# Last output block copied in halves by two engines, and two output blocks stored by one DMA

## The chip, the cores and the metric

The kernel runs on one core of a Trainium2 chip. The metric is the time of one execution on the device in microseconds; lower is better. TensorE (PE) multiplies matrices and leaves the results in PSUM, an accumulator memory of eight banks. VectorE (DVE), ScalarE (ACT) and GpSimd (POOL) do the rest, and SyncE (SP) issues the transfers between the chip's working memory and HBM. The transfers are carried out by 16 DMA engines.

## The reference

Four sequences of 768 positions go through a linear attention with a decaying state (8 heads of 48), and its result, viewed as 768 rows of 384 values per sequence, through a gated long convolution. In short:

```python
# attention: state is updated at each position t
y[t]  = r[t] @ (state + (u * k[t]) outer v[t])
state = w[t] * state + k[t] outer v[t]
# gated convolution over the sequence, per sequence x = y of all heads side by side
x1, x2, x3 = split(x @ w_proj, 3)                      # 384 columns each
x2c = irfft(rfft(x2) * rfft(filter))                   # along the 768 positions
out = (x1 * x2c * x3) @ w_out                          # 768 x 384, float32
```

The inputs and the output are float32; the output has 4 x 768 x 384 values.

## The kernel before, in words

Each sequence (batch index 0 to 3) is cut into six row blocks of 128 positions. The attention runs block by block over 24 blocks in all; the convolution is done with matrices of sines and cosines on TensorE. Work of one sequence's convolution overlaps with the attention of the next ones, so only the convolution of the last sequence (index 3) is left for the end of the program.

There is no scheduler. The order is written out by hand in the string ORDER, one word for each step: the engine's letter (P for TensorE, A for ScalarE, V for VectorE, G for GpSimd, S for the queue of SP), the step and its indices, and behind an @ the PSUM bank. Each engine carries out its words in the order in which they stand. The waits between engines are put in by the framework, from which tile each instruction reads and writes; the order does not name them.

The steps that the change and the prediction touch are at the end of the program, for sequence 3:

- `yl` and `yh` (lines 817 and 822) multiply the convolution's result by the gate, the left and the right half of the positions, for each of three column groups. Their results are the left factors of the output product.
- `pA.3.t` (line 835) starts the output product of row block t with the first two column groups; `pB.3.t` (line 842) adds the third. `pA.3.4` is special: it makes one PSUM tile of two banks in the pool `wide`, and puts row block 4 into its first bank and row block 5 into its second. The other blocks have a bank each.
- `o.3.t` (the copy helper, line 276 on ScalarE and 278 on VectorE) copies row block t, 128 partitions by 384 float32 values, from PSUM into the tile `o_all`, which holds six such blocks. The previous sequence used the same tile, so a copy must also wait until the old block's store has landed.
- `st.3.t` (line 859) stores row block t of `o_all` to HBM with one DMA of 192 KB on the queue of SP.

The last words of the order for ScalarE are the copies of blocks 2, 1, 5, 3 and 4; VectorE copies block 0. The last stores are those of blocks 2, 1, 5, 3, 4 and 0, in this order. When the last has landed, the engines pass a closing barrier and the program ends.

Of the kernel before, what the change touches and what calls it, by code (L numbers as in the profile page):

```python
# [19 lines left out]
B, H, S, D = 4, 8, 768, 48  # L20
L = 128
NCH = S // L
C = H * D
# [112 lines left out]
P:po.2.3@3 V:s.3.0 V:s.3.1 P:iE.3.2@2 G:yl.3.0 A:o.2.3 P:iO.3.2@5 V:d.3.0 A:o.2.1 P:iP.3.2  # L136
S:st.2.3 V:yl.3.1 G:yh.3.0 P:po.2.5@3 S:st.2.1 V:d.3.1 A:ec.3.2 P:po.2.4@4 A:o.2.5 V:s.3.2
P:pA.3.1@1 A:o.2.4 S:st.2.5 P:pA.3.2@0 V:yl.3.2 V:yh.3.1 S:st.2.4 P:pB.3.2 V:d.3.2 P:pB.3.1
P:pA.3.4@8 A:o.3.2 V:yh.3.2 A:o.3.1 S:st.3.2 P:pB.3.4 S:st.3.1 P:pA.3.3@2 A:o.3.5 P:pB.3.3
P:pA.3.0@3 A:o.3.3 S:st.3.5 P:pB.3.0 A:o.3.4 V:o.3.0 S:st.3.3 S:st.3.4 S:st.3.0  # L140
"""


# [1 line left out]
def kernel(  # L145
# [12 lines left out]
    nc = tc.nc  # L158
# [54 lines left out]
    o_all = consts.tile([L, NCH, C], FP32)  # L213
# [39 lines left out]
    bank_of = {}  # L253
# [20 lines left out]
    def copy(e, o, i):  # L274
        if e == "A":
            nc.scalar.activation(out=o, in_=i, func=AF.Copy)  # L276
        elif e == "V":
            nc.vector.tensor_copy(out=o, in_=i)  # L278
        else:
            nc.gpsimd.tensor_copy(out=o, in_=i)  # L280
# [574 lines left out]
    def op_o(e, b, ti):  # L855
        copy(e, o_all[:, ti, :], bank_of[f"po.{b}.{ti}"])

    def op_st(e, b, ti):
        nc.sync.dma_start(out=out[b, ti * L:(ti + 1) * L, :], in_=o_all[:, ti, :])

# [71 lines left out]
```

## Time and profile before

| | |
|---|---|
| time, median of 3 runs | 156.67 us (156.21 to 157.68) |
| the profiled execution's own time | 157.1 us |
| its span, from the first to the last instruction | 155.4 us |
| mean granted TensorE clock | 0.973 |
| DMA queues: bytes moved | 28.98 MB, mean 186 GB/s |
| stores of the output | 24 of 192 KB each, median 2.2 us from issue to landing |

The profile shows one execution. Its times are in microseconds from the span's start, and a row of the timeline gives start, duration, engine, line, operation, the tile written and the tiles read. In brackets stands how long the engine was idle before, and what ended the idle time. SPq is the queue of SP: the duration of its rows is the time to issue a transfer, not the transfer. PE, DVE, ACT and POOL are TensorE, VectorE, ScalarE and GpSimd. The profiled execution is one of many, so a sum made from its rows is made against its own 155.4 and 157.1 us, and is then set beside the median.

### The profile page before, as it was taken

To read this page: it belongs to the slowest core of one execution; us is meant where nothing else is said; L and a number is where in the kernel's file an instruction comes from. 1 tells how busy PE (TensorE), PEld (TensorE's weight loads), DVE (VectorE), ACT (ScalarE), POOL (GpSimd) and SP (SyncE) were. 2 spreads that over 40 slices of the span, in tenths; PEclk is the share of its full clock that TensorE was granted. 3 is DMA by queue.
4 is the path that set the end of the run, shared out by engine and by line. 5 is a ranking of instruction groups with operands and counts; after the bars stand their busy time and mean duration, and the time that the engine had idled before them with its cause. 6 is when DMAs were issued, how large, how long until landed. Compare 5 with 4: busy or idle time off the path is not lost.

```text
span 155.4 us, 4177 instructions
## 1 busy us (share of the span) xinstructions
PE 144.5 (93%) x1540; PEld 90.8 (58%) x1540; DVE 138.3 (89%) x264; ACT 128.2 (82%) x306; POOL 115.9 (75%) x134
## 2 busy tenths in 40 slices
PE   6969988968999999999999999999999999999990
PEld 3446565756465666656757666775666566555440
DVE  6537879979989999999999999999999989999950
ACT  3279659969698899989999999999999877677470
POOL 7200869892999899799969999699999998900600
PEclk9985799999999999999999999999999999999997
DMA  5999979999999999899999999978999986000575
GB/s 96 196 202 183 207 148 197 195 286 226 244 172 281 253 178 200 170 192 211 190 200 259 170 181 210 189 147 141 227 209 228 206 175 222 2 0 0 181 281 203
DMA packets 112038, 28.98 MB, mean 186 GB/s; under 512 B 106641, under 2 KB 112018, under 8 KB 112018
## 3 DMA queue, kind: packets, MB, share of 16 engines
q1 hardware_dynamic: 112018, 28.72, 84.4%
q8 instruction: 12, 0.20, 0.6%
q14 instruction: 8, 0.07, 0.1%
HBM read 22.41 MB, written 4.72 MB: 175 GB/s over the span
## 4 chain that ended last, share of the span: by engine, by line
PE 63%; DMA 12%; DVE 11%; ACT 5%; SPq 5%; issue 2%; DVEq 0%
PE p L705 13%; DMA ldw<-in_w_dram 9%; PE x L735 6%; PE po L850 6%; PE f L421 5%; SPq L452 5%; PE sc L607 3%; PE f L413 3%; PE tqk L588 3%; DMA ldv<-in_v_dram 3%; PE iE L792 3%; PE iO L781 3%; PE iE L781 2%; PE yt L675 2%; DVE mt L614 2%
## 5 line engine op out<-in xcount | busy, mean ns | idle before, releaser
L505 POOL TENSOR_TENSOR qk<-ldr,eq 128x384 bf16<-128x384 f32 x20 | 21.3, 1067 | 11.4 <-ACT F L357 10.3
L705 PE MATMUL p<-xT,wproj 128*128 128x384 bf16 x144 | 29.3, 326 | 0.1
L614 DVE TENSOR_TENSOR mt<-sc,mask_excl 128x1024 bf16<-128x1024 f32 x24 | 29.2, 1216 | 0.0
L502 POOL TENSOR_TENSOR qk<-ldk,en 128x384 bf16<-128x384 f32 x21 | 22.4, 1067 | 4.1 <-PE kv L625 2.7
L508 POOL TENSOR_TENSOR rk<-ldr,ldk 128x384 bf16<-128x384 f32 x19 | 19.8, 1042 | 1.8 <-issue 1.5
L560 POOL TENSOR_TENSOR rku<-rk,u_bc 128x384 bf16<-128x384 bf16 x19 | 18.0, 945 | 2.5 <-DVE rk L508 1.3
L462 ACT ACTIVATE lg<-ldw 128x384 bf16<-128x384 f32 x24 | 12.6, 530 | 8.6 <-DMA ldw<-in_w_dram 7.5
L705 PEld LDWEIGHTS <-wproj 128*128 128x128 bf16 x144 | 13.0, 97 | 8.2 <-issue 1.0
L582 POOL TENSOR_TENSOR vc<-v,cc 128x384 bf16<-128x384 bf16 x19 | 16.5, 867 | 0.7 <-DVE cc L566 0.5
L757 DVE TENSOR_TENSOR filt<-f,HF 128x768 bf16<-128x768 f32 x18 | 16.6, 952 | 0.1
L735 PE MATMUL x<-wproj,sd 128*128 128x384 bf16 x72 | 14.9, 326 | 0.3 <-DVE HF L435 0.2
L276 ACT ACTIVATE qkT<-tqk 128x1024 bf16<-128x1024 bf16 x13 | 13.3, 1027 | 0.1
L276 ACT ACTIVATE v<-ldv 128x384 bf16<-128x384 f32 x23 | 12.2, 530 | 1.3 <-DMA ldv<-in_v_dram 1.3
L276 ACT ACTIVATE x<-p 128x384 bf16<-128x384 f32 x24 | 11.7, 499 | 1.8 <-PE p L705 1.6
L726 POOL TENSOR_TENSOR g<-g,x 128x384 bf16<-128x384 bf16 x8 | 7.1, 912 | 8.1 <-DVE g L278 8.1
L276 ACT ACTIVATE ab<-x 128x384 bf16<-128x384 f32 x24 | 11.7, 500 | 1.2 <-PE x L735 0.9
L484 ACT ACTIVATE en<-cs 128x384 f32<-128x384 f32 x24 | 11.9, 500 | 0.9 <-PE cs L466 0.7
L490 ACT ACTIVATE eq<-ce 128x384 f32<-128x384 f32 x24 | 11.5, 494 | 0.6 <-PE ce L478 0.6
L588 PE MATMUL tqk<-ident,qk 128*128 128x128 bf16 x144 | 11.5, 230 | 0.2 <-ACT phi L496 0.2
L632 DVE TENSOR_TENSOR S<-kv,phi 128x384 bf16<-128x384 f32 x20 | 10.9, 550 | 0.3 <-PE kv L625 0.2
L566 DVE TENSOR_REDUCE cc<-rku 128x8 f32<-128x384 bf16 x21 | 11.1, 541 | 0.0
L276 ACT ACTIVATE xT<-yt 128x384 bf16<-128x384 bf16 x20 | 9.9, 495 | 1.3 <-PE yt L675 0.6
(158 smaller groups left out, 397.0 us busy)
## 6 DMA issues: line engine op xcount, KB each, us to landing
ldw<-in_w_dram SPq DMA_DIRECT2D x24, 192.0 KB, 4.0
ldk<-in_k_dram SPq DMA_DIRECT2D x24, 192.0 KB, 4.2
ldr<-in_r_dram SPq DMA_DIRECT2D x24, 192.0 KB, 3.9
ldv<-in_v_dram SPq DMA_DIRECT2D x24, 192.0 KB, 4.0
out_dram<-o_all SPq DMA_DIRECT2D x24, 192.0 KB, 2.2
raw<-in_moe_w_proj_dram SPq DMA_DIRECT2D x3, 576.0 KB, 5.8
filt<-in_moe_filter_fft_dram SPq DMA_DIRECT2D x1, 1152.0 KB
P<-in_moe_w_out_dram SPq DMA_DIRECT2D x1, 576.0 KB, 5.0
```

The source lines that it names most:

```text
L276: nc.scalar.activation(out=o, in_=i, func=AF.Copy)
L462: nc.scalar.activation(out=o, in_=i, func=AF.Ln)
L502: two(e).tensor_mul(qk_b[c % 3][:, 1, :, 0:D], ld["k"][c % 6], en_b[c % 3])
L505: two(e).tensor_mul(qk_b[c % 3][:, 0, :, 0:D], ld["r"][c % 6], eq_b[c % 3])
L508: two(e).tensor_mul(rk_b[c % 2], ld["r"][c % 6], ld["k"][c % 6])
L560: two(e).tensor_mul(rku_b[c % 2], rk_b[c % 2], u_bc)
L582: two(e).tensor_mul(o, v, s.to_broadcast([L, H, D]))
L588: nc.tensor.transpose(p[:, x, j, :], qk_b[c % 3][:, x, 2 * j:2 * j + 2, :], ident)
L614: nc.vector.tensor_mul(mt_b[c % 3], bank_of[f"sc{c}"].rearrange("p q j t -> p (q j) t"), dataclasses.replace(m[:, :], ap=[m[:, :].ap[0], [ ...
L705: nc.tensor.matmul(p, wproj[:, cb, col0:col0 + L], xT_b[b % 2][:, cb, sl], start=(cb == 0), stop=(cb == CB - 1),)
L735: nc.tensor.matmul(p, sd_b[q][0][:, cb, ti * L:(ti + 1) * L], wproj[:, cb, C:2 * C], start=(cb == 0), stop=(cb == CB - 1),)
L757: two(e).tensor_mul(U_all[:, part, n], dataclasses.replace(f, ap=[f.ap[0], [0, 2]] + list(f.ap[1:])), HF[:, n, part:part + 2, :],)
```

## The change

The last words of the order are rewritten, and two steps are added. `oh` copies one half of the columns (192 of 384) of a row block; `sp` stores row blocks 4 and 5 of a sequence with one DMA of 384 KB.

- Block 5 is copied by VectorE instead of ScalarE (`V:o.3.5`).
- ScalarE copies block 4 ahead of block 3 instead of behind it.
- Blocks 4 and 5 are stored by one DMA (`S:sp.3`), which stands ahead of the store of block 3.
- Block 0 is copied in two halves, the left by ScalarE, the right by VectorE.

```diff
-P:pA.3.4@8 A:o.3.2 V:yh.3.2 A:o.3.1 S:st.3.2 P:pB.3.4 S:st.3.1 P:pA.3.3@2 A:o.3.5 P:pB.3.3
-P:pA.3.0@3 A:o.3.3 S:st.3.5 P:pB.3.0 A:o.3.4 V:o.3.0 S:st.3.3 S:st.3.4 S:st.3.0
+P:pA.3.4@8 A:o.3.2 V:yh.3.2 A:o.3.1 S:st.3.2 P:pB.3.4 S:st.3.1 P:pA.3.3@2 V:o.3.5 A:o.3.4 P:pB.3.3
+P:pA.3.0@3 S:sp.3 A:o.3.3 P:pB.3.0 S:st.3.3 A:oh.3.0.0 V:oh.3.0.1 S:st.3.0
...
+    def op_oh(e, b, ti, n):
+        sl = slice(n * (C // 2), (n + 1) * (C // 2))
+        copy(e, o_all[:, ti, sl], bank_of[f"po.{b}.{ti}"][:, sl])
+
+    def op_sp(e, b):
+        nc.sync.dma_start(
+            out=out[b, 4 * L:, :].rearrange("(a p) c -> p a c", p=L), in_=o_all[:, 4:, :]
+        )
```

## The prediction

> **What bounds the kernel now.** I read the page first, then the chain that ended last, because the change touches only the last two lines of the written order. The page says that over the whole span several engines are nearly full:
>
> ```profile
> span 155.4 us, 4177 instructions
> PE 144.5 (93%) x1540; PEld 90.8 (58%) x1540; DVE 138.3 (89%) x264; ACT 128.2 (82%) x306; POOL 115.9 (75%) x134
> ```
>
> These shares say nothing about the tail, which has limits of its own. The end of the chain, in order of time (start, duration, what):
>
> ```profile
> 150.68 0.33 PE pA L835 x2
> 151.00 0.18 PE pA L842
> 151.18 0.02 issue
> 151.20 0.56 DVE o_all L278
> ```
>
> The chain as printed stops at the last copy, 151.76, but the span runs 3.6 us further. So the next views were the timeline of each engine in that stretch, the queue's own waits, and busy time by short stretches. Here are the last copies, with the last two VectorE multiplies before them (start, duration, engine, line, operation):
>
> ```profile
> 148.43 0.35 DVE L822 TENSOR_TENSOR raw<-raw,g 128x384 bf16<-128x384 bf16 x1
> 149.28 0.36 DVE L822 TENSOR_TENSOR raw<-raw,g 128x384 bf16<-128x384 bf16 x1
> 149.69 0.50 PE L842 MATMUL pA<-wout,raw 128*128 128x384 bf16 x2
> 150.30 0.49 ACT L276 ACTIVATE o_all<-pA 128x384 f32<-128x384 f32 x1 [0.39 <-PE pA L842]
> 150.72 0.49 ACT L276 ACTIVATE o_all<-pA 128x384 f32<-128x384 f32 x1
> 151.10 0.48 ACT L276 ACTIVATE o_all<-pA 128x384 f32<-128x384 f32 x1
> 151.20 0.56 DVE L278 COPY o_all<-pA 128x384 f32<-128x384 f32 x1 [1.57 <-PE pA L842]
> ```
>
> ScalarE copies row blocks 5, 3 and 4 one behind the other (150.30, 150.72, 151.10), VectorE copies block 0. Each is followed by its store on SP's queue:
>
> ```profile
> 150.81 0.33 SPq L859 DMA_DIRECT2D out_dram<-o_all  x1
> 151.24 0.38 SPq L859 DMA_DIRECT2D out_dram<-o_all  x1
> 151.71 0.40 SPq L859 DMA_DIRECT2D out_dram<-o_all  x1
> 152.21 0.41 SPq L859 DMA_DIRECT2D out_dram<-o_all  x1
> ```
>
> The first is issued 0.02 us after the copy of block 5 ends (150.79). The last is issued 0.45 us after its copy ended (151.76), so it waited for SP, which needs 0.43 to 0.50 us from one store to the next. Whether SP or the engines that move the data set the end is seen in the stretches (engine columns, then granted clock, DMA share, GB/s):
>
> ```profile
> 148.80:149.15 0.35, 0.35 (x4) 0.22 (x3) 0.35 (x1) 0.16 (x1) 0.00 (x0) 1.00 0.04 13
> 149.15:150.20 1.05, 1.05 (x8) 0.43 (x7) 0.45 (x2) 0.76 (x2) 0.00 (x0) 1.00 0.96 358
> 151.40:151.60 0.20, 0.00 (x0) 0.00 (x0) 0.20 (x1) 0.19 (x1) 0.00 (x0) 1.00 0.26 85
> 151.60:151.80 0.20, 0.00 (x0) 0.00 (x0) 0.16 (x1) 0.00 (x0) 0.00 (x0) 1.00 0.68 253
> 151.80:153.60 1.80, 0.00 (x0) 0.00 (x0) 0.00 (x0) 0.00 (x0) 0.00 (x0) 1.00 1.00 367
> 153.60:153.80 0.20, 0.00 (x0) 0.00 (x0) 0.00 (x0) 0.00 (x0) 0.00 (x0) 1.00 0.88 346
> 153.80:154.00 0.20, 0.00 (x0) 0.00 (x0) 0.00 (x0) 0.00 (x0) 0.00 (x0) 0.58 0.11 31
> ```
>
> Near 151.6 the DMA engines are almost out of work (share 0.26); from about 151.65 to 153.83 they are full at 367 GB/s and empty after that. Summing these rows from 151.60 on gives 50.6 + 660.6 + 69.2 + 6.2 = 787 KB, which is four stores of 192 KB (196.6 thousand bytes each). So the four last stores leave no gap: **the tail is bound by the bytes, counted from the moment the first of the four stores is issued.** The landing times confirm it (the store's issue with min/median/max in ns, then us from issue to landing):
>
> ```profile
> L859 SPq DMA_DIRECT2D out_dram<-o_all x1: 332/332/332, 150.8 to 150.8; - x1
> DMA to landing us min/median/max: 1.9/1.9/1.9
> ...
> L859 SPq DMA_DIRECT2D out_dram<-o_all x2: 399/406/412, 151.7 to 152.2; - x2
> DMA to landing us min/median/max: 2.1/2.1/2.1
> ...
> L927 SPq EVENT_SEMAPHORE  x7: 17/28/28, 154.3 to 155.3; - x7
> ```
>
> The first of the four lands 1.9 us after its issue, the last two after 2.1: each queues a little behind the one before. The last lands at 152.21 + 2.1 = 154.31, and there the closing steps of SP begin. From the first issue to the last landing it is 154.31 - 150.81 = **3.50 us**; the remaining 1.1 us to the span's end is closing work that the change does not touch.
>
> **The change part by part.** Nothing ahead of the last two lines of the order moves; the first 150.2 us stay as they are, and TensorE's instructions are the same to the end.
>
> *Block 5 to VectorE.* VectorE is free from 149.28 + 0.36 = 149.64. The two last matmuls that write blocks 4 and 5 begin at 149.69 and end at 150.19. The copy also needs the old store from this row block to have landed; that was issued at 148.32, 1.9 us earlier than 150.22:
>
> ```profile
> 148.32 0.33 SPq L859 DMA_DIRECT2D out_dram<-o_all  x1
> ```
>
> So VectorE starts at about 150.25 and, at the 0.56 us of the same copy of block 0, ends at 150.81. ScalarE's copy ended at 150.79, so this edit is nearly free by itself.
>
> *Block 4 behind block 5.* The two blocks lie in one PSUM tile of two banks, and in the changed program as built ScalarE's copy of block 4 waits for VectorE's counter at the very value that the copy of block 5 raises. The copies that look parallel run one after the other. The hand-over from VectorE costs about 0.05 us (multiply ends 149.64, the matmul behind it starts 149.69), up to the 0.11 between matmul end 150.19 and copy start 150.30. Block 4 therefore starts at 150.81 + 0.07 = 150.88 and ends, at 0.49, at 151.37. Queued behind it on ScalarE are block 3 and the half of block 0. Were the wait not there, block 4 would still need its old store, issued third from last before the tail, to land:
>
> ```profile
> 148.74 1.10 SPq L859 DMA_DIRECT2D out_dram<-o_all  x2
> ...
> L859 SPq DMA_DIRECT2D out_dram<-o_all x4: 332/358/402, 148.7 to 150.8; - x4
> DMA to landing us min/median/max: 1.9/1.9/2.0
> ```
>
> That is 150.64 to 150.74, so it could start at 150.76 and end at 151.25 at best. This is the low bound for this step.
>
> *One store for blocks 4 and 5.* Today's store of block 5 goes out at 150.81, while block 4 is still uncopied. The paired store must wait for both and goes out at 151.37 + 0.02, say 151.40: **0.59 us later** (0.46 at the low bound). The engines have nothing else to move by then, so the short gap at 151.5 grows by as much. An operation like the pair has no row in this trace. Its issue lies between one block (0.33) and the three blocks of a weight load:
>
> ```profile
> L386 SPq DMA_DIRECT2D P<-in_moe_w_out_dram x1: 672/672/672, 79.9 to 79.9; - x1
> ```
>
> Halfway is 0.50, that is 0.17 more. The data of the lone store issued at 148.32 began to flow near 149.15, 0.50 us after its issue ended; if data wait for the whole issue, the pair is 0.17 late, if they flow while it runs, 0. I take the middle, **0.08**. The pair carries the same bytes in the same 1,536-byte rows, and the engines are full at 367 GB/s, so I cost the data themselves at nothing, with bounds from the fastest to the slowest row: none better than 367, and the span's mean of 186 GB/s (loads and stores mixed) below.
>
> ```profile
> DMA packets 112038, 28.98 MB, mean 186 GB/s; under 512 B 106641, under 2 KB 112018, under 8 KB 112018
> ```
>
> At 186 the pair's 393 KB would take 2.11 us instead of 1.07: up to 1.04 more. I stay by the nearer row, the stores of the tail.
>
> *Block 3 later.* Its copy moves behind block 4, from 150.72 to about 151.27 (ScalarE starts one copy 0.38 to 0.42 us after another), ending 151.76. SP finishes the pair's issue at 151.90 and needs some 0.09 between stores (151.24 + 0.38 to 151.71), so block 3 goes out at about 151.99; its data would be ready at 152.82 while the pair is still moving until 153.4. Hidden behind the pair; without that cover it would cost its own 0.74 (from 151.24).
>
> *The last block in halves.* Neither half has a row. Between the tiny copies and the full ones (count, then busy us and mean ns of one)
>
> ```profile
> L276 ACT ACTIVATE cc<-cp 128x8 f32<-128x8 f32 x2 | 0.3, 175 | 0.0
> L276 ACT ACTIVATE o_all<-pA 128x384 f32<-128x384 f32 x5 | 2.2, 490 | 0.7 <-PE pA L842 0.4 <-ACT o_all L276 0.3
> L278 DVE COPY cc<-cp 128x8 f32<-128x8 f32 x1 | 0.2, 167 | 1.0 <-PE cp L554 1.0
> L278 DVE COPY o_all<-pA 128x384 f32<-128x384 f32 x1 | 0.6, 557 | 1.6 <-PE pA L842 1.6
> ```
>
> 192 columns come out, by straight lines, at 0.33 us on ScalarE and 0.36 on VectorE; the bounds are the rows themselves. The word "at once" does not hold either: in the built program VectorE's half waits for the value of ScalarE's counter that the first half raises. ScalarE's half runs from about 151.67 to 152.00, VectorE's from 152.05 to 152.41, against 151.76 for the single copy today. But SP is free for the last store only at 151.99 + 0.40 + 0.09 = 152.48, so the serial halves hide behind SP's queue, and SP behind the engines: data of the last block would be ready at 153.3 and the engines reach it at about 153.9. If both covers were gone, the halves would cost 0.65. Behind the last half nothing waits but this store.
>
> The Trainium skill, page "PSUM — Partial Sum Buffer", section "PSUM bank collisions raise a hardware error", says that two engines may not touch one bank on the same partitions in one cycle, reads against reads included, so that a dependency is put between them. Block 0 lies in one bank, so by that rule its halves cannot overlap whatever the order says; two engines free to read it at once would be done at 152.03. No run here shows such a pair overlapping; by both readings the sum is the same, and the rule lowers the chance of the third rival below.
>
> *One store and one semaphore less* saves SP about 0.47 us once, in a queue that is not the limit, and one of seven short closing waits (17 to 28 ns): nothing.
>
> **Sum.** 0.59 + 0.08 = 0.67 us. With 3.50 us from the first issue to the last landing kept, the end is 151.40 + 0.08 + 3.50 = 154.98 against 154.31. The profiled span becomes 156.1; the profiled execution took 157.1 in all, 1.7 outside the span, and would become 157.8. It lies 0.4 above the median of 156.67, so the forecast on the median is 156.67 + 0.67 = **157.3 us**, 0.4% more. Own bounds: 0.46 to 0.59 + 0.04 + 0.17 = 0.80.
>
> The Trainium skill, page "DMA: Bandwidth & Descriptors", sections "Rules for kernel authors" and "Specifications", wants 1 MiB or more per DMA for full bandwidth and names a ceiling of 435 GB/s. By that ceiling the 787 KB would take 1.81 us instead of 2.15, and the forecast would be 157.0; the trace shows the engines already full at 367 with single blocks, which speaks against it.
>
> **Rivals.**
> 1. *SP's queue sets the end, not the bytes.* Then only the last issue counts: 152.48 instead of 152.21, and 1.9 to landing instead of 2.1: +0.07, time 156.7. For it: SP needs 0.43 to 0.50 per store, nearly the 0.54 that the engines take for 196.6 KB. Against: share 1.00 for 1.8 us, and landings that grow from 1.9 to 2.1. Chance 0.20.
> 2. *The paired store flows slower than two.* With the 1.04 above: 0.67 + 1.04 = 1.71, time 158.4. For it: rows of the output 196 KB apart in one transfer, of which the tail has no example. Against: same row size, same number of rows. Chance 0.10.
> 3. *Not slower: copies overlap and the freed slot on SP counts.* If both engines copied at once, the pair would go out at 151.27, block 3 at 151.27 + 0.47 = 151.74, block 0 at 152.21 at a landing of 1.9: 0.2 less than before, time 156.5. It decides from the point at which the last store is issued by 152.2 and finds the engines free. Against it stand the waits in the built program and the full engines. That the change does not do what it says is, by those waits, my expectation for the copies. Chance 0.08.
>
> **How the numbers follow.** The forecast keeps 0.62. About 1% (1.6 us) is what a measurement of this kernel can tell from no change; the three runs shown spread from 156.21 to 157.68. With that spread the forecast and rivals 1 and 3 fall almost wholly within 1% (0.62 less 0.04 that end above, 0.20, and 0.06), rival 2 lies on the bound (0.07 above, 0.03 within), and 0.02 of rival 3 falls below. So faster 0.02, same 0.87, slower 0.11. The range goes from rival 3 less 0.3 to just short of rival 2: 156.2 to 158.2; above it lies most of rival 2 and below it almost nothing.
>
> **What would show it.** Right: VectorE's copy of block 5 ends near 150.8, ScalarE's copy of block 4 starts only after it, the pair is issued near 151.4, DMA share falls to zero around 151.5 to 152.2 and then stays at 1.00 for 2.2 us, the last landing near 155.0, and VectorE's half starts after ScalarE's has ended. Wrong: a pair issued before 151.2 (no wait, or a faster hand-over), data of the pair at clearly less or more than 367 GB/s, gaps in the DMA share behind the pair (then SP sets the end), or any change before 150 us.

## The result, and the profile after

The changed kernel takes 158.38 us (median of 16 runs, 157.22 to 158.63), the kernel before in the same sessions 157.12 us (16 runs, 156.21 to 158.49). The ratio of the means is 1.0067, interval 1.0039 to 1.0095: 0.7% more, or about 1.05 us. A kernel read 1.0041 against itself in a later session, so this ratio alone does not settle that the change costs time; the profiles, and all the ratios taken together, are what the following rests on. The forecast was 0.67 us, a ratio of 1.0043, inside that interval; the 157.3 us that it gave on the median of the first three runs is 1.1 below the later median, partly because the median of before had moved up too, by 0.45. For the same reason 158.38 lies just above the upper end of the range, 158.2, which was laid around the earlier median.

The last copies of the changed kernel, as the timeline of each engine has them, headed by the line with the span:

```profile
core 0 of [0], span 156.5 us
...
149.44 0.36 DVE L822 TENSOR_TENSOR raw<-raw,g 128x384 bf16<-128x384 bf16 x1
149.85 0.50 PE L842 MATMUL pA<-wout,raw 128*128 128x384 bf16 x2
150.72 0.56 DVE L278 COPY o_all<-pA 128x384 f32<-128x384 f32 x1 [0.93 <-DMA out_dram<-o_all]
151.36 0.49 ACT L276 ACTIVATE o_all<-pA 128x384 f32<-128x384 f32 x1 [0.87 <-DVE o_all L278]
151.75 0.48 ACT L276 ACTIVATE o_all<-pA 128x384 f32<-128x384 f32 x1
152.12 0.34 ACT L276 ACTIVATE o_all<-pA 128x192 f32<-128x192 f32 x1
152.49 0.36 DVE L278 COPY o_all<-pA 128x192 f32<-128x192 f32 x1 [1.21 <-ACT o_all L276]
```

VectorE's copy of block 5 begins at 150.72, 0.37 us after TensorE has finished the block (149.85 + 0.50 = 150.35), and the bracket names a DMA as what it waited for: the old store from the same rows. ScalarE's copy of block 4 begins 0.08 us after VectorE's has ended (151.28), and names VectorE. VectorE's half of block 0 begins 0.03 us after ScalarE's half has ended (152.46), and names ScalarE. So nothing that the order puts side by side runs side by side. The stores then, again from the timeline:

```profile
151.88 0.38 SPq L863 DMA_DIRECT2D out_dram<-o_all  x1
152.36 0.98 SPq L868 DMA_DIRECT2D out_dram<-o_all  x2
```

The pair goes out at 151.88, where the store of block 5 went out at 150.81 before. The busy time by stretches shows what that does to the DMA engines (last two columns: their share and GB/s):

```profile
151.40:151.80 0.40, 0.00 (x0) 0.00 (x0) 0.00 (x0) 0.40 (x2) 0.00 (x0) 1.00 0.96 361
151.80:152.00 0.20, 0.00 (x0) 0.00 (x0) 0.00 (x0) 0.20 (x2) 0.00 (x0) 1.00 0.59 215
152.00:152.20 0.20, 0.00 (x0) 0.00 (x0) 0.00 (x0) 0.20 (x2) 0.00 (x0) 1.00 0.01 0
152.20:152.40 0.20, 0.00 (x0) 0.00 (x0) 0.00 (x0) 0.20 (x2) 0.00 (x0) 1.00 0.00 0
152.40:152.60 0.20, 0.00 (x0) 0.00 (x0) 0.11 (x1) 0.06 (x1) 0.00 (x0) 1.00 0.00 0
152.60:154.00 1.40, 0.00 (x0) 0.00 (x0) 0.25 (x1) 0.00 (x0) 0.00 (x0) 1.00 0.86 315
154.40:154.60 0.20, 0.00 (x0) 0.00 (x0) 0.00 (x0) 0.00 (x0) 0.00 (x0) 1.00 1.02 369
154.80:155.00 0.20, 0.00 (x0) 0.00 (x0) 0.00 (x0) 0.00 (x0) 0.00 (x0) 0.50 0.64 231
```

From about 151.9 to 152.8 they have nothing to move; then the four blocks pass at full rate, as before, and the end comes where that stream ends. The gap is 0.9 us here; before it was about 0.2 (the rows from 151.40 to 151.80 of the kernel before).

Two numbers carry the rest. The first is from the start of VectorE's last multiply (line 822, the step that releases the product of blocks 4 and 5) to the first issue of the last four blocks: 150.81 - 149.28 = 1.53 before, 151.88 - 149.44 = 2.44 after. The second is from that issue to the span's end: 155.4 - 150.81 = 4.59 before, 156.5 - 151.88 = 4.62 after. The first has 0.91 us of the difference, and the 0.03 in the second is less than the span's rounding to 0.1 us. Counting from the multiply leaves out the body, which the change does not touch and which moves from run to run: the multiply starts at 147.65 in one profile and between 148.99 and 149.67 in the others.

### The profile page after: what moved, and what is told of

Read it like the earlier page. It is cut to its first block, busy times and chain, and to the rows that moved or that the text cites. A ratio compares the mean times of both kernels' runs of the same rounds, so it can differ in the third digit from the quotient of the medians.

```text
span 156.5 us, 4177 instructions
## 1 busy us (share of the span) xinstructions
PE 143.6 (92%) x1540; PEld 90.5 (58%) x1540; DVE 139.7 (89%) x265; ACT 128.0 (82%) x306; POOL 115.8 (74%) x134
## 4 chain that ended last, share of the span: by engine, by line
PE 68%; DVE 11%; DMA 7%; ACT 6%; SPq 3%; issue 3%; ACTq 0%; DVEq 0%
PE p L705 13%; PE x L735 6%; PE po L850 6%; PE f L421 5%; PE tqk L588 4%; PE sc L607 4%; DMA ldv<-in_v_dram 3%; PE f L413 3%; SPq L452 3%; PE iE L792 3%; DMA ldw<-in_w_dram 3%; PE cp L269 3%; PE iO L781 3%; PE yt L675 2%; PE iE L781 2%
```

## The experiments

Theory A is the prediction's: the pair goes out late, and the end follows the first issue at a fixed distance because the DMA engines are full from there. Theory B: SP's queue and the serial halves set the end. Theory C: the loss lies ahead of the last copies. The ratios below are against the kernel before in the same sessions.

**Two stores instead of the pair.** The copies stay as changed.

```diff
-P:pA.3.0@3 S:sp.3 A:o.3.3 P:pB.3.0 S:st.3.3 ...
+P:pA.3.0@3 S:st.3.5 A:o.3.3 P:pB.3.0 S:st.3.4 S:st.3.3 ...
```

> The changed kernel, but blocks 5 and 4 are stored by two DMAs again, each right behind its copy; copies as changed (block 5 by VectorE, block 4 behind it on ScalarE, block 0 in halves). Theory A (the pair is issued late, and the end lies 3.5 us behind the first issue of the last four blocks, the engines being full from there): the first issue follows the copy of block 5 instead of block 4, 0.55 to 0.6 us earlier than in the changed kernel, so 0.5 to 0.6 us faster than it and 0.1 to 0.5 slower than before (the old store of block 5 lands 0.0 to 0.45 later than in the run of before). Theory B (SP's queue and the serial halves set the last issue): the halves still end near 152.85 and four stores need 0.47 each, so no gain over the changed kernel. Theory C (the loss lies ahead of the last copies, in the body or in the first stores of sequence 2): no gain over the changed kernel either, and PE's last matmul ends 0.2 to 0.4 us later than before.

Ratio 1.0016 (0.9984 to 1.0047). The timeline:

```profile
148.99 0.36 DVE L822 TENSOR_TENSOR raw<-raw,g 128x384 bf16<-128x384 bf16 x1
150.00 0.56 DVE L278 COPY o_all<-pA 128x384 f32<-128x384 f32 x1 [0.65 <-PE pA L842]
150.64 1.09 ACT L276 ACTIVATE o_all<-pA 128x384 f32<-128x384 f32 x3 [1.06 <-DVE o_all L278]
150.59 0.33 SPq L868 DMA_DIRECT2D out_dram<-o_all  x1
```

The first issue is 1.60 us behind the multiply, almost as before, and the span ends 4.61 behind it (155.2). Serial copies, serial halves and all, the tail is only 0.1 us longer than before. That is Theory A; B and C had it stay at the changed kernel's. The copy of block 5 waits for TensorE here and for no DMA, although its order and waits are those of the changed kernel: more on this below.

**The pair alone**, on the kernel before: ScalarE copies 5, 4, 3, VectorE the whole of block 0.

```diff
-... A:o.3.5 P:pB.3.3
-P:pA.3.0@3 A:o.3.3 S:st.3.5 P:pB.3.0 A:o.3.4 V:o.3.0 S:st.3.3 S:st.3.4 S:st.3.0
+... A:o.3.5 A:o.3.4 P:pB.3.3
+P:pA.3.0@3 S:sp.3 A:o.3.3 P:pB.3.0 V:o.3.0 S:st.3.3 S:st.3.0
```

> The kernel before with the pair alone: ScalarE copies 5, 4, 3 in this order, VectorE the whole of block 0, blocks 4 and 5 stored by one DMA. Theory A: the pair goes out behind ScalarE's second copy, 0.42 us (one copy's start to the next) later than the store of block 5, so 0.4 to 0.5 us slower than before (0.3%). Theory B: the last issue is 151.22 + 2 x 0.48 = 152.2, as before: no change, or 0.1 faster. Theory C: no change against before.

Ratio 1.0032 (0.9999 to 1.0065). Timeline:

```profile
149.09 0.36 DVE L822 TENSOR_TENSOR raw<-raw,g 128x384 bf16<-128x384 bf16 x1
150.99 0.38 SPq L863 DMA_DIRECT2D out_dram<-o_all  x1
```

The pair goes out 1.90 behind the multiply, 0.37 later than the store of block 5 before; the span ends 4.61 behind the issue (155.6). Waiting for the second block is the first part of the loss, and it needs neither VectorE nor the halves.

**The halves alone**, on the kernel before.

```diff
-... A:o.3.4 V:o.3.0 S:st.3.3 S:st.3.4 S:st.3.0
+... A:o.3.4 S:st.3.3 S:st.3.4 A:oh.3.0.0 V:oh.3.0.1 S:st.3.0
```

> The kernel before with the halves alone: ScalarE copies 5, 3, 4 and then the left half of block 0, VectorE the right half; all stores single, in the old order. The halves run one behind the other and the second ends about 152.2, where SP becomes free for the last store. Theory A: no change against before (within 0.1 us). Theory B: up to 0.1 us slower, more if VectorE's half is handed over slower than 0.05 us. Theory C: no change.

Ratio 0.9988 (0.9944 to 1.0033). VectorE's half ends at 151.84 + 0.36 = 152.20 and SP issues the last store at 152.26, its queue's turn, as forecast. First issue 1.69 behind the multiply, span's end 4.56 behind that. The halves cost nothing that can be seen, and gain nothing.

**A tile for each of blocks 4 and 5**, on the changed kernel, so that their copies do not wait for each other.

```diff
+            for t, bk in ((4, bank), (5, 8)):
+                bank_of[f"po.{b}.{t}"] = ps(f"pA.{b}.{t}", bk)
...
-P:pA.3.4@8
+P:pA.3.4@4
```

> The changed kernel, but row blocks 4 and 5 are accumulated in two PSUM tiles of their own (banks of the two pools) instead of one tile of two banks, so that ScalarE's copy of block 4 waits for TensorE and no longer for VectorE's copy of block 5. Theory A: both copies run at once; the pair goes out 0.25 to 0.6 us earlier than in the changed kernel (as far as the old store of block 4 lets ScalarE begin), and the time is 0.3 to 0.6 us less than the changed kernel's, 0.4 to 0.7 more than before. Theory B: the halves move along with ScalarE, so 0.3 to 0.6 less too. Theory C: no gain.

Ratio 1.0052 (1.0020 to 1.0085). Timeline:

```profile
149.54 0.36 DVE L822 TENSOR_TENSOR raw<-raw,g 128x384 bf16<-128x384 bf16 x1
150.54 0.56 DVE L278 COPY o_all<-pA 128x384 f32<-128x384 f32 x1 [0.65 <-PE pA L841]
150.86 1.09 ACT L276 ACTIVATE o_all<-pA 128x384 f32<-128x384 f32 x3 [0.74 <-DMA out_dram<-o_all]
151.38 0.38 SPq L862 DMA_DIRECT2D out_dram<-o_all  x1
```

ScalarE now begins while VectorE still copies, held by the old store of block 4 alone, and the pair goes out 1.84 behind the multiply; the span ends 4.52 behind that (155.9). By the profile the shared tile is worth about 0.3 us (2.16 with it, in the two runs below). The timed ratio is 0.24 us below the changed kernel's and 0.8 above before, where 0.3 to 0.6 and 0.4 to 0.7 were expected; its interval is 1.0 us wide, three times the gain, so it shows neither.

**A buffer of their own for blocks 4 and 5**, on the changed kernel, so that their copies wait for no old store.

```diff
+    o_end = consts.tile([L, 2, C], FP32)
...
+        return o_end[:, ti - 4, :] if b == 3 and ti >= 4 else o_all[:, ti, :]
...
-            out=..., in_=o_all[:, 4:, :]
+            out=..., in_=o_end
```

> The changed kernel, but blocks 4 and 5 of the last sequence are copied into a buffer of their own, so that their copies no longer wait for the old stores from the same rows to land. Theory A: VectorE's copy of block 5 starts 0.05 us behind the last matmul of that block instead of at the landing (in the run of the changed kernel 150.40 instead of 150.72), the pair goes out 0.3 us earlier and the time is 0.3 us less than the changed kernel's, 0.6 more than before. Theory B: the halves and SP move along, so 0.2 to 0.3 less too. Theory C: no gain.

Ratio 1.0082 (1.0040 to 1.0123). In the profile VectorE's copy starts at 150.62, 0.04 behind TensorE, and the pair goes out 2.06 behind the multiply (149.67 to 151.73), 0.38 earlier than in the first profile of the changed kernel. The span ends 4.57 behind that. The expected gain is in the tail of the profile. The time does not show it: the ratio stands for 1.3 us over before, where 0.6 was expected. The multiply itself starts at 149.67 in this run, 0.2 and 0.6 later than in the two profiles of the changed kernel; whether the buffer did that or the run is open.

**The store of sequence 1's block 5 earlier.** The wait for the old store goes back through a chain: in the order, this store stands behind the first store of sequence 2, on a queue that has issued nothing for about 15 us; its landing releases ScalarE's copy of block 5 of sequence 2, whose own store is the old store in question. Moved to the other stores of sequence 1, it lands long before. Tried on both kernels:

```diff
-... V:cc23 S:st.1.0 V:cc22 ...
+... V:cc23 S:st.1.0 S:st.1.5 V:cc22 ...
...
-S:st.2.2 P:iP.3.0 V:g.3.2.1 S:st.1.5 G:g.3.1.1 ...
+S:st.2.2 P:iP.3.0 V:g.3.2.1 G:g.3.1.1 ...
```

> The kernel before, with the store of block 5 of sequence 1 issued right behind the other stores of that sequence (near 129 us) instead of behind the first store of sequence 2 (near 144 us), where it lands 3.0 to 3.9 us after its issue and holds up the copy of block 5 of sequence 2, and with it the old store that the copy of block 5 of sequence 3 waits for. Theory A with the chain of old stores: that copy starts 0.05 to 0.1 us behind TensorE in every run, the first of the four last stores goes out 0 to 0.2 us earlier and the time is 0 to 0.3 us less than before. Theory C: whatever the queue's first stores cost stays, no change.

> The changed kernel with the same earlier store. Theory A with the chain of old stores: VectorE's copy of block 5 starts at 0.05 us behind TensorE instead of 0.37, the pair goes out 0.3 us earlier (about 1.2 us behind the last matmul of blocks 4 and 5 instead of 1.53), and the time is 0.3 less than the changed kernel's, 0.7 more than before. If the wait for the old store was a chance of one profiled run: no gain over the changed kernel.

On the kernel before: ratio 0.9991 (0.9959 to 1.0024), first issue 1.52 behind the multiply, as in its first profile: no gain. On the changed kernel: ratio 1.0049 (1.0017 to 1.0081), and the timeline

```profile
149.07 0.36 DVE L822 TENSOR_TENSOR raw<-raw,g 128x384 bf16<-128x384 bf16 x1
150.08 0.56 DVE L278 COPY o_all<-pA 128x384 f32<-128x384 f32 x1 [0.65 <-PE pA L842]
150.72 1.09 ACT L276 ACTIVATE o_all<-pA 128x384 f32<-128x384 f32 x3 [0.77 <-DVE o_all L278]
151.23 0.38 SPq L863 DMA_DIRECT2D out_dram<-o_all  x1
```

has the copy right behind TensorE and the pair 2.16 behind the multiply. Against the same edit on the kernel before that is 2.16 - 1.52 = 0.64 us, with the spans' ends at 4.57 behind the first issue in both. This pair of runs is the change without any old store in the way. The time lies 0.77 us over before, near the 0.7 expected, but by a ratio that the spread of the measurement could give as well.

**Block 0 ahead of blocks 4 and 5**, on the kernel before with the earlier store: an attempt at a faster version.

```diff
-P:pA.3.4@8 ...
-P:pA.3.0@3 A:o.3.3 S:st.3.5 P:pB.3.0 ...
+P:pA.3.0@3 P:pB.3.0 P:pA.3.4@8 ... P:pA.3.3@2 V:o.3.0 S:st.3.0 A:o.3.5 P:pB.3.3
+S:st.3.5 V:o.3.3 A:o.3.4 S:st.3.4 S:st.3.3
```

> A version built on Theory A: the kernel before with the earlier store of e7, and the output product of block 0 ahead of that of blocks 4 and 5, so that its store fills the gaps in which the DMA engines have no work (two gaps of about 0.1 and 0.25 us near 150.3 and 151.5). VectorE copies blocks 0 and 3, ScalarE 5 and 4, stores in the order 0, 5, 4, 3. If the bytes bind the tail, the gaps close and the end lies 0.2 to 0.4 us earlier than before; if SP's cadence of 0.47 us and the last copy bind, the gain is 0 to 0.2.

Ratio 1.0013 (0.9986 to 1.0041): no faster. From the multiply to the span's end it takes 155.2 - 149.19 = 6.01 us, against 155.4 - 149.28 = 6.12 before. That is the smaller of the two gains named, but not for the reason given with it, SP's cadence. The bytes still bind. The last store goes out at 151.99, so its data could have begun by about 152.85 (0.83 to 0.86 after the issue of a single store), while the engines, busy in every stretch from 151.0 to 153.6 (share 0.87 to 1.03), reach it only near 153.2 (an estimate: their data end at 153.7, and a block takes 0.54 at 367 GB/s). The gap near 151.5 has closed, as meant. But the store ahead of the four goes out 0.87 behind the multiply (150.06) instead of 0.66 (149.94 before), and the earlier gap has grown (share 0.06 from 150.0 to 150.2; before 0.39 from 150.2 to 150.4), so the stream as a whole starts later and little is won. Why that store goes out later was not followed up.

**Both kernels once more**, unchanged, for a second profile and for the width of the measurement.

> The changed kernel itself, profiled a second time, to see whether the wait for the old store (0.37 us behind TensorE in its first profile, absent in the run with two stores) belongs to it or to the run. If it goes with the landing of the first stores of sequence 2: a landing of 3.5 us or less there, and VectorE's copy of block 5 starts less than 0.1 us behind TensorE, the pair goes out about 2.15 us behind the start of VectorE's last multiply; at 3.8 us or more, about 2.45 as in the first profile. If it belongs to the kernel: 2.45 whatever the first stores do.

> The kernel before itself as a kernel of a job, a second profile and a measure of what no change reads: ratio 1.000, with the spread of the intervals seen so far (0.003). The first of the last four stores goes out about 1.5 us behind the start of VectorE's last multiply when the first stores of sequence 2 land in 3.5 us or less, 1.7 when they take 3.8 or more.

The second profile of the changed kernel, first the timeline, then the landing of the store of sequence 1's block 5 (us from issue, shown by line and window) in this run and in the first:

```profile
149.06 0.36 DVE L822 TENSOR_TENSOR raw<-raw,g 128x384 bf16<-128x384 bf16 x1
150.07 0.56 DVE L278 COPY o_all<-pA 128x384 f32<-128x384 f32 x1 [0.65 <-PE pA L842]
151.22 0.38 SPq L863 DMA_DIRECT2D out_dram<-o_all  x1
```

```profile
L868 SPq DMA_DIRECT2D out_dram<-o_all x1: 425/425/425, 143.9 to 143.9; - x1
DMA to landing us min/median/max: 3.4/3.4/3.4
```

```profile
L868 SPq DMA_DIRECT2D out_dram<-o_all x1: 424/424/424, 144.3 to 144.3; - x1
DMA to landing us min/median/max: 3.9/3.9/3.9
```

With a landing of 3.4 the copy of block 5 follows TensorE at once and the pair goes out 2.16 behind the multiply; with 3.9 it was 2.44. The wait for the old store goes with the run. The kernel before shows the same in its second profile: landing 3.8, first issue at 149.34, 1.69 behind the multiply, against 1.53 with 3.6. Both are what the expectation named.

The ratios were 1.0064 (1.0032 to 1.0097) for the changed kernel and 1.0041 (1.0002 to 1.0079) for the kernel before **against itself**. So a ratio of 0.4% is within what no change reads here, and what is said of the parts rests on the profiles, not on their timed ratios. Taken together the ratios still sort: the six kernels with the pair, the changed one among them, read 1.0032 to 1.0082 (mean 1.0058), the five without it 0.9988 to 1.0041 (mean 1.0010), and in each of the three later sessions every kernel with the pair reads above every one without it. The difference of the means is 0.48%, or about 0.75 us.

All profiled executions together, in us:

| kernel | store of sequence 1's block 5, to landing | multiply to first issue of the last four blocks | first issue to span's end |
|---|---|---|---|
| before | 3.6 | 1.53 | 4.59 |
| before, second profile | 3.8 | 1.69 | 4.56 |
| before, earlier store | out of the way | 1.52 | 4.57 |
| halves alone | 3.8 | 1.69 | 4.56 |
| copies as changed, two stores | 3.1 | 1.60 | 4.61 |
| pair alone | 3.5 | 1.90 | 4.61 |
| changed, own tiles | 2.9 | 1.84 | 4.52 |
| changed, own buffer | no matter | 2.06 | 4.57 |
| changed, earlier store | out of the way | 2.16 | 4.57 |
| changed, second profile | 3.4 | 2.16 | 4.58 |
| changed | 3.9 | 2.44 | 4.62 |
| before, earlier store, block 0 first | out of the way | 1.30 | 4.71 |

The span is printed to 0.1 us, so the last column is good to about 0.05. Without the last row it spans 0.1 us while the one before it spans 0.9. Whether one or two blocks are in the first store, whole copies or halves, makes no difference to it. The last row shows where the rule ends: there the first of the four stores is issued while the store ahead of it still has its data to move, so there is no gap in front of it, its data wait in the queue (they begin 0.97 us after the issue), and the distance is longer by that.

## Why the prediction was right, point by point

*What bounds the tail*: right. Eleven of twelve profiles have the end at 4.52 to 4.62 us behind the first issue of the last four blocks; in the twelfth (block 0 first, 4.71) the engines are full as well, but that issue has no gap in front of it.

*Block 5 to VectorE*: "nearly free by itself" holds when the old store has landed (copy start 0.08 to 0.10 us behind TensorE in the runs with an early landing, 0.04 with a buffer of its own). I took its landing from one run as a fixed 150.22, a near tie with TensorE, and gave no bound for a later one. In the first profile of the changed kernel the old store was issued at 148.74 and landed 1.9 us later, near 150.64, which cost 0.28 us (2.44 against 2.16). This is the one term of the sum that was left out. The kernel before has the same wait (0.16 in its second profile), so it is a cost of the run more than of the change.

*Block 4 behind block 5*: right. Hand-over 0.08 us, forecast 0.07; copies serial in the shared tile, side by side in tiles of their own. What kept them apart was the shared tile: the two blocks lie in two banks.

*One store for two blocks*: the delay of the first issue was forecast at 0.59; without an old store in the way it is 2.16 - 1.53 = 0.63. Of this, 0.37 comes from waiting for a second copy at all (pair alone) and the other 0.26 from handing the first copy to VectorE, with the copies one behind the other. The extra 0.08 for the pair's longer issue was not seen in the end. The issue took 0.38 us, not 0.50. By the packets in the traces the pair's data do begin 0.89 to 0.91 us after its issue, a single store's 0.83 to 0.86 (the run with block 0 first left out), but the distance to the span's end is the same with the pair (4.52 to 4.62) as without (4.56 to 4.61). The two slips, 0.04 too little and 0.08 too much, nearly cancel: 0.63 against 0.67. That the sum came out so near is luck to that extent.

*Block 3 later*: right. Its store goes out 0.48 us behind the pair (152.36 - 151.88; forecast 0.59) and is hidden behind it. The price without that cover is 0.75 by the prediction's own times (151.99 - 151.24), not 0.74; nothing rests on it.

*Halves*: right. They ran one behind the other, 0.34 and 0.36 us long (forecast 0.33 and 0.36), and cost nothing at the end. "Hidden behind SP's queue" is a tie, though: in the changed kernel the second half ends at 152.85 and the last store goes out at 152.88, 0.10 us after SP has ended its issue before (152.78). In the run with two stores the half is the later one (its end 152.13, the store 152.16, SP's issue before ended 151.99), and the end still does not move: the data ahead of the last block cover it. Whether two engines could have read the one bank at once was not tried, since the framework's wait stands in every version of the halves.

*The rivals*: SP's queue as the bound falls with the two-store run, which has the serial halves and one store more and gains back 0.5 to 0.85 us (6.21 from the multiply to the span's end, against 6.74 and 7.06). The last issue does not set the end either: from it to the span's end it takes about 3.1 us in the profiles without the pair (155.4 - 152.21 before) and about 3.6 in those with it (156.5 - 152.88 changed). A slower flow of the pair falls with the last column of the table. Overlapping copies were made with own tiles, and the tail was still 0.2 longer than before (6.36 against 6.12 from the multiply to the span's end).

What stays open: the timed ratio of 1.0067 stands for 1.05 us, the tail explains 0.5 to 0.9 (0.94 between the first profiles of the two kernels, 0.62 for the second profile of the changed kernel against the first of before, and about 0.5 against its second), and the ratios taken together give 0.75. With a kernel reading 1.0041 against itself, the rest is not an effect that these runs can name.

## What to carry to other kernels

At the end of a kernel whose last transfers run back to back, count from the issue of the first one behind the last gap in the DMA engines' work: merging stores helps only if the merged store can leave as early as the first one did. Two engines that read one PSUM tile took turns here, even in different banks, so read the waits of the built program before counting on an overlap. And when a copy waits for an old store from the same buffer, follow that chain back: a store that was merely put late in the order can decide when the last one starts.

## What the runs showed of the hardware that was not expected

The first stores of sequence 2, issued after about 15 us in which SP's queue issued nothing, landed 2.9 to 3.9 us after their issue, where the same 192 KB stores at the end of the kernel before took 1.9 to 2.1, and that differed from run to run of the same program (3.9 and 3.4 for the changed kernel). The traces point at the cause, though no run varied it. The page of the changed kernel lists, beside the queue of the data, this one (packets, MB, share of the 16 engines):

```profile
q8 instruction: 12, 0.20, 0.5%
```

These are 12 packets of 16 KB, and in every one of the twelve profiles one of them begins 0.2 to 0.8 us after the issue of the second of these stores (sequence 1's block 5, where it was not moved) and takes 0.9 to 1.7 us. Where the packet ends 1.08 us after that issue, the store lands after 2.9 (own tiles); 1.54 goes with 3.4 and 2.07 with 3.9 (the two profiles of the changed kernel). In all twelve the landing comes 1.7 to 1.9 us after the packet's end. Meanwhile the DMA share falls to 0.05 to 0.06 (146.1 to 146.9 in the first profile of the changed kernel), which is what one engine of the 16 gives. An estimate from this: one engine is held up by the packet and then moves its part of the stores alone. The pause of the queue is not needed for it: in the profile of before a store issued at 128.8, right behind others, took 4.1 us to land, and another of these packets ran from 130.1 to 131.7.

A store of 384 KB in rows of 1,536 bytes took SP 0.38 us to issue, no more than many of 192 KB (0.33 to 0.47), and its data began 0.9 us after the issue, only some 0.06 later than those of the smaller one.
